# q and v of two pairs of heads in one load, a unit matrix copied on the chip, and a longer written order

## The chip, the cores and the metric

The kernel runs on one core of one Trainium2 chip. A core has five engines with a queue of instructions each: TensorE (PE, with its weight loads shown apart as PEld), VectorE (DVE), ScalarE (ACT), GpSimd (POOL) and SyncE (SP), which in this kernel issues all data transfers. Sixteen DMA engines move the data. Engines wait for each other through semaphores only, and each works through its own queue in order. The metric is the device time of one execution in microseconds (us).

## The reference

Three stages, one after the other, all in float32:

```python
# attention, B=4, H=8, S=576, D=64: heads 0-3 see the last 32 positions,
# heads 4-7 every fourth of the last 128
attn = softmax(where(mask, q @ k.T / 8, -1e9));  x = (attn @ v) as (2304, 512)
# soft mixture of 8 experts with 4 slots each
logits = x @ phi                                 # (2304, 32)
slots = softmax(logits, over tokens).T @ x       # (32, 512)
out_e = relu(slots_e @ w1[e]) @ w2[e]            # 8 experts, 512 -> 1024 -> 512
x = softmax(logits, over slots) @ out            # (2304, 512)
# gated layer
h = x @ w_in; out = (h * sigmoid(h)) @ w_out     # 512 -> 2048 -> 512
```

## The kernel before, in words

**Attention.** The 32 heads are worked off as 16 pairs n, the two heads of a pair on 64 partitions each. The loads of a pair are `lq`, `lk`, `lv`, each 128 rows of 576 floats (2304 B a row, 288 KB). POOL and DVE spread q into a block form (`qx`, `qy`) and mask v (`vx`, `vy`); PE puts the mask (`M`) and the scores (`S`) into PSUM; DVE takes the row maxima (`rm`), ACT the exponentials (`ex`, nine a pair), DVE the reciprocals (`rc`), POOL normalises (`nm`), DVE transposes in 32x32 blocks (`pt`), PE multiplies by v (`pv`). ACT copies the result out (`xe`), PE transposes it with a unit matrix (`T`) and computes the logits (`lt`), ACT stores x (`te`). q, v and k lie in slots that are used again: q in four, v in four (two towards the end), k in five, later three. A load into a slot waits until the spreading of the pair that was there is over.

**Experts.** After each fourth pair the running softmax over tokens is brought up to date (`da` to `ds`, `dc` its matrix products) and the softmax over slots prepared (`caa` to `cag`, then transposes `cb` on PE). After the last pair PE runs 16 steps `L1.i` over w1 and 16 steps `L2.i` over w2, each with a weight of 1 MB that a load `lw1.i` or `lw2.i` brings. The last of these, `L2.15`, is cut in three (`L2a`, `L2b`, `L2.15`: 256, 128 and 128 columns) with three loads.

**Gated layer.** The expert outputs (`soe`, `sotm`, `sote`) are multiplied with blocks of w_in (`aqh0`, `aq0` for the first 128 columns, `aqr0` for the next), copied out on ACT (`ah`) with a rest on DVE (`al`), and then `h` (PE), `gh` and `si` (ACT), `gl` (DVE), `on` and `om` (PE) run over the first third of the tokens; the other two thirds follow with `ch`, `cs`, `sh`, `sl`, `pp`. w_in and w_out come in a packed form that DVE unpacks (`cva`, `cvb`, `cvi`, and `cvc`, `cvd`, `cvo`). The first part of w_in is loaded in two halves (`lwi0.0`, `lwi0.1`).

**What sets the order.** Every step above is an operation with an engine, an estimated cost and a list of what it needs. All instructions are emitted in one order, and each engine gets its own in that order. The kernel before lets a list scheduler (`list_schedule`) find the order up to step `L2.5`, and takes the rest from the table `LATER`. The loads have an order of their own (`loads`, steered by the string `ATT`).

The change touches `qraw`, `vraw`, `load_q`, `load_v` (L126 to L184), the loop that declares the operations of a pair (L332 to L373), the load of the unit matrix (L1174, `cip`: 128 rows with phi and a float32 unit matrix side by side in tile `ip`), the list of loads (L1186 to L1199), `LATER`, and the layout of the inputs in `lay`.

Of the kernel before, what the change touches and what calls it, by code (L numbers as in the profile page):

```python
# [27 lines left out]
JH = 6  # L28
CBANK = ((2, 1), (5, 1), (4, 6), (5, 1))
# [3 lines left out]
def fused_kernel(ctx: ExitStack, tc: tile.TileContext, a: dict):  # L33
# [45 lines left out]
    def reg(key, off, n):  # L79
        return tiles[key][:, off:off + n]  # L80
# [38 lines left out]
    def before(slot, n):  # L119
        return max((m for m in range(n) if slot(m) == slot(n)), default=None)  # L120
# [47 lines left out]

    def load_q(n):
        b, p = divmod(n, 4)  # L170
        sp.dma_start(out=qraw(n), in_=a["q"][b, p])
# [160 lines left out]
    for n in range(NPAIR):  # L332
        b, p = divmod(n, 4)
        kb, rb = before(kslot, n), before(rslot, n)
        qb, vb = before(qslot, n), rb if n < NPAIR - 1 else None
        op(f"lk{n}", "SP", .74, [f"S{kb}"] if kb is not None else [], lambda n=n: load_k(n))
        op(f"lq{n}", "SP", .74, [f"qx{qb}", f"qy{qb}"] if qb is not None else [], lambda n=n: load_q(n))
        op(f"lv{n}", "SP", .74, [f"vx{vb}", f"vy{vb}"] if vb is not None else [], lambda n=n: load_v(n))
        for z in range(2):
            op(f"q{'xy'[z]}{n}", "DVE" if z and n not in QP else "POOL", .7, [f"lq{n}", f"S{n-2}" if n >= 2 else None], lambda n=n, z=z: spread(n, z))  # L340
        for z in range(2):
            op(f"v{'xy'[z]}{n}", veng(n) if z else "POOL", {"POOL": 1.4, "ACT": .68, "DVE": .745}[veng(n) if z else "POOL"], [f"lv{n}", f"pv{n-2}.1" if n >= 2 else "izm", ("nm0", "rc0")[z] if n == 1 else None], lambda n=n, z=z: vmask(n, z))
# [28 lines left out]
        op(f"T{n}", "PE", .56, ["cip", f"xe{n}", f"te{n-1}" if n else None], lambda n=n: tmm(n))  # L371
# [453 lines left out]
    op("ani", "ACT", .25, ["L2.6", "cip"], ani)  # L825
# [348 lines left out]
    op("cip", "SP", .37, [], lambda: sp.dma_start(out=ip, in_=a["ip"]))  # L1174
# [6 lines left out]
    op("crs", "POOL", .9, ["cip", "nm3"], crs)  # L1181
# [340 lines left out]
```

## Time and profile before

| | |
|---|---|
| median of 3 runs | 344.35 us (343.3 to 344.42) |
| the profiled execution | 343.64 us, its span from first to last instruction 341.5 us |
| granted TensorE clock | 1.000 of full speed |
| PE busy | 329.4 us, 96% of the span |
| DVE, ACT, POOL busy | 263.3, 221.9, 74.6 us |
| moved by DMA | 70.03 MB, nearly all in the first 145 us |

The span has three parts: attention until about 97 us, the experts until about 131 us, and the gated layer. The page's forty slices (8.5 us each) show the DMA engines full in slices 2 to 16, and PE nearly full throughout. A PE that is called busy is not always at its peak, since ends of matmuls are modelled. So an idle stretch of PE is a lower bound, and the weight loads (PEld), whose starts are measured, tell more exactly when PE had to wait. "[0.34 <-DMA x]" behind a row means that the engine stood idle for 0.34 us before it and that what came last was the transfer into x; "issue" means that it waited for nothing the profile shows.

### The profile page before, as it was taken

The page shows a single profiled execution, that of the slowest core. Times are in us where ns is not written, and L with a number is a line of the kernel's source. Part 1 is how long each engine was busy: PE and PEld are TensorE (multiplying, and loading weights), DVE is VectorE, ACT ScalarE, POOL GpSimd, SP SyncE. Part 2 cuts the span into 40 slices and gives each one's busy share as a digit, 9 for nine tenths or more (in the row PEclk, how much of TensorE's full clock was granted, in tenths as well). Part 3 has the DMA queues.
Part 4 walks back from the last instruction along what each step waited for, and adds up shares of the span by engine and source line. Part 5 has one row for each costly group of instructions (what it writes and reads, how often), then busy time and mean ns, then how long its engine had stood idle before and what let it go on. Part 6 is the DMA issues. An engine that isn't in the chain of part 4 may idle for free.

```text
span 341.5 us, 8179 instructions
## 1 busy us (share of the span) xinstructions
PE 329.4 (96%) x3221; PEld 272.1 (80%) x3232; DVE 263.3 (77%) x479; ACT 221.9 (65%) x639; POOL 74.6 (22%) x121
## 2 busy tenths in 40 slices
PE   7998999999899999999999999999999999999995
PEld 3687877777633337788888888999999999999995
DVE  5777877689660099999999997989994654999573
ACT  3599989797430125778496999996467666645540
POOL 6987978675260000000000000000000000000000
PEclk9999999999999999999999999999999999999999
DMA  7999999999999999818390000110200011000004
GB/s 259 405 405 406 403 401 407 416 404 415 416 405 423 416 411 419 349 58 322 125 356 15 0 0 2 55 68 2 77 3 0 0 71 69 3 23 23 2 22 147
DMA packets 17893, 70.03 MB, mean 205 GB/s; under 512 B 1984, under 2 KB 4288, under 8 KB 12096
## 3 DMA queue, kind: packets, MB, share of 16 engines
q1 hardware_dynamic: 17856, 69.53, 51.9%
q8 instruction: 25, 0.41, 0.5%
q14 instruction: 12, 0.10, 0.1%
HBM read 64.80 MB, written 4.72 MB: 204 GB/s over the span
## 4 chain that ended last, share of the span: by engine, by line
PE 83%; DMA 8%; DVE 3%; ACT 2%; POOL 1%; issue 1%; DVEq 0%; ACTq 0%; POOLq 0%
PE ps L86 80%; DMA w_w2.13_1760<-in_w 5%; PE ps L312 3%; DMA w_wi<-in_w_in 3%; ACT rt_px L232 1%; DMA rs_raw<-in_q 1%; POOL rv_v L1138 1%; ACT rt_px L301 1%; POOL rb_a L180 0%; PE ps L434 0%; POOL ra_a L180 0%; ACT x_xb L315 0%; DVE stats L227 0%; DVE csm L413 0%; DVE spaced L244 0%
## 5 line engine op out<-in xcount | busy, mean ns | idle before, releaser
L1083 DVE TENSOR_TENSOR rt_stl<-w_raww,rs_sth 128x768 fp32r<-128x768 f32 (+1 forms) x52 | 42.2, 830 | 18.2 <-ACT rs_sth L1081 17.9
L86 PE MATMUL ps<-w_ws,x_gz 128*128 128x512 f32 x216 | 53.6, 393 | 0.0
L86 PE MATMUL ps<-rs_sth,w_ws 128*128 128x384 f32 x192 | 53.1, 334 | 0.0
L1081 ACT CAST rs_sth<-w_raww 128x768 fp32r<-128x768 f32 (+1 forms) x52 | 37.8, 738 | 22.3 <-PE ps L86 16.6
L232 ACT ACTIVATE rt_px<-ps,spaced 128x64 f32<-128x64 f32 x144 | 43.5, 332 | 10.2 <-DVE spaced L228 8.5
L86 PEld LDWEIGHTS ps<-w_ws,x_gz 128*128 128x128 f32 x216 | 40.0, 188 | 7.7 <-issue 0.4
L86 PEld LDWEIGHTS ps<-rs_sth,w_ws 128*128 128x128 f32 x192 | 35.1, 188 | 0.0
L232 ACT ACTIVATION_READ_ACCUMULATOR rt_px<-ps,spaced 128x1 f32 x144 | 32.3, 225 | 0.0
L86 PE MATMUL ps<-rt_stl,w_ws 128*128 128x384 f32 x96 | 32.1, 334 | 0.0
L86 PE MATMUL ps<-ct_ct,rv_astk 128*128 128x384 f32 x96 | 27.3, 338 | 0.0
L1066 ACT ACTIVATE w_raww<-ps 128x384 f32<-128x384 f32 x48 | 22.0, 493 | 7.1 <-PE ps L86 7.0
L249 POOL TENSOR_TENSOR rt_px<-rt_px,stats 128x576 f32<-128x576 f32 (+2 forms) x17 | 18.6, 1093 | 8.2 <-DVE stats L245 3.4
L86 PEld LDWEIGHTS ps<-ct_ct,rv_astk 128*128 128x128 f32 x96 | 17.6, 188 | 2.4 <-issue 0.4
L86 PEld LDWEIGHTS ps<-rt_stl,w_ws 128*128 128x128 f32 x96 | 18.0, 188 | 0.0
L896 ACT ACTIVATE x_gz<-ps 128x768 fp32r<-128x768 f32 (+3 forms) x18 | 13.3, 740 | 4.8 <-PE ps L86 4.7
L899 DVE TENSOR_TENSOR x_gz<-rt_gtm,x_gz 128x768 fp32r<-128x768 f32 (+3 forms) x18 | 15.5, 864 | 1.0 <-ACT rt_gtm L889 0.9
L1081 ACT CAST rs_sth<-x_rawx 128x768 fp32r<-128x768 f32 x12 | 10.0, 837 | 9.6 <-PE ps L86 6.3
L889 ACT ACTIVATE rt_gtm<-ps 128x768 f32<-128x768 f32 (+3 forms) x18 | 13.2, 742 | 3.8 <-PE ps L86 3.6
L86 PEld LDWEIGHTS ps<-ra_a,rv_v 128*64 128x64 f32 x320 | 13.3, 137 | 2.8 <-issue 1.1
L86 PE MATMUL ps<-ra_a,rv_v 128*64 128x96 f32 (+2 forms) x320 | 14.9, 241 | 0.4 <-DVE ra_a L263 0.3
L1083 DVE TENSOR_TENSOR rt_stl<-x_rawx,rs_sth 128x768 fp32r<-128x768 f32 x12 | 11.5, 954 | 4.7 <-ACT rs_sth L1081 4.6
L315 ACT COPY x_xb<-ps 128x640 f32<-128x640 f32 x16 | 11.3, 708 | 5.7 <-PE ps L312 3.5
(298 smaller groups left out, 772.2 us busy)
## 6 DMA issues: line engine op xcount, KB each, us to landing
w_wi<-in_w_in SPq DMA_DIRECT2D x7, 1024.0 KB, 7.1
rs_wo<-in_w_out SPq DMA_DIRECT2D x4, 1024.0 KB, 5.8
rk_k<-in_k SPq DMA_DIRECT2D x12, 288.0 KB, 7.6
w_wo<-in_w_out SPq DMA_DIRECT2D x3, 1024.0 KB, 4.7
rs_raw<-in_v SPq DMA_DIRECT2D x9, 288.0 KB, 9.4
rs_raw<-in_q SPq DMA_DIRECT2D x8, 288.0 KB, 6.5
w_more<-in_q SPq DMA_DIRECT2D x8, 288.0 KB, 9.4
w_more<-in_v SPq DMA_DIRECT2D x6, 288.0 KB, 8.0
```

Source lines behind the costliest of these rows:

```text
L86: pe.matmul(out, lhsT=lhsT, rhs=rhs, start=start, stop=stop, skip_group_check=True)
L232: act.activation(out=preg(n)[:, j, :], in_=sj(n, j), func=ACTF.Exp, scale=D ** -0.5, bias=nmx[:, r, j // 3, j % 3:j % 3 + 1], accum_out=su ...
L249: pool.tensor_tensor(out=p, in0=p, in1=rinv[:, n % 2, j0:j1].rearrange("p (j o) -> p j o", o=1).to_broadcast([128, j1 - j0, 64]), op=ALU.mult)
L301: act.copy(out=x, in_=src)
L312: pe.transpose(ps[0:m, c:c + 128], x[:, 128 * t:128 * t + m], ident)
L315: act.copy(out=xreg(n)[:, :, 0:128], in_=ps[:, TC:TC + 640].rearrange("p (t c) -> p t c", c=128))
L889: act.activation(out=cols(gt(f), x), in_=hbs(x), func=ACTF.Silu)
L896: act.activation(out=cols(gbuf(f, 0), x), in_=hbs(x), func=ACTF.Silu)
L899: dve.tensor_tensor(out=gsl(gbuf(f, 1), x), in0=gsl(gt(f), x), in1=gsl(gbuf(f, 0), x), op=ALU.subtract)
L1066: op(f"cs{x}", "ACT", .385, [f"ch{x}", *d], lambda c=c, b=b, i=i, s=s: act.activation(out=at(c, b, i), in_=bank[6 + s][:, 0:TW], func=ACTF ...
L1081: op(f"sh{x}", "ACT", cost(c, PRODS[p][0], j, .42, .74), [*src, old, "cvo14" if o < 0 else None], lambda c=c, p=p, j=j: both(c, p, j, 0, l ...
L1083: lambda c=c, p=p, j=j: both(c, p, j, 1, lambda x, h, l: dve.tensor_tensor(out=l, in0=x, in1=h, op=ALU.subtract)))
```

## The change

1. q of pairs 2n and 2n+1 lie side by side in the input, 128 rows of 4608 B. From pair 2 on one load brings both, into two neighbouring slots; it waits until both are free. The same for v of pairs 2 to 13. Pairs 0 and 1, and v of pairs 14 and 15, are still loaded alone. That makes 7 double loads of q and 6 of v in place of 26 single ones.
2. The float32 unit matrix is no longer loaded. `cip` brings phi alone (128 rows of 512 B instead of 1024 B), and a new step `idn` on DVE copies the bfloat16 unit matrix, which comes with the mask, into float32.
3. `LATER` holds the whole order but for its first 37 operations, those of the start. The order of the loads comes from it as well.

```diff
+VLAST = NPAIR - 2
...
-    def qraw(n):
+    def qraw(n, m=1):
         i = qslot(n)
-        return reg("raw", 576 * i, 576) if i < 2 else reg("more0", 576 * (i - 2), 576)
+        return reg("raw", 576 * i, 576 * m) if i < 2 else reg("more0", 576 * (i - 2), 576 * m)
...
+    def lead(n, last):
+
+        return n if n < 2 or n >= last else n - n % 2
+
+    def load_two(raw, src, n, last):
+
+        x, y = src[n // 2], raw(n)
+        if lead(n + 1, last) != n:
+            sp.dma_start(out=y, in_=x[:, S * (n % 2):S * (n % 2) + S])
+        else:
+            sp.dma_start(out=raw(n, 2), in_=x)
+
     def load_q(n):
-        b, p = divmod(n, 4)
-        sp.dma_start(out=qraw(n), in_=a["q"][b, p])
+        load_two(qraw, a["q"], n, NPAIR)
...
     def load_v(n):
-        b, p = divmod(n, 4)
-        sp.dma_start(out=vraw(n), in_=a["v"][b, p])
+        load_two(vraw, a["v"], n, VLAST)
...
-        op(f"T{n}", "PE", .56, ["cip", f"xe{n}", f"te{n-1}" if n else None], lambda n=n: tmm(n))
+        op(f"T{n}", "PE", .56, ["idn", f"xe{n}", f"te{n-1}" if n else None], lambda n=n: tmm(n))
...
-    op("cip", "SP", .37, [], lambda: sp.dma_start(out=ip, in_=a["ip"]))
+    op("cip", "SP", .21, [], lambda: sp.dma_start(out=ip[:, 0:128], in_=a["phi"]))
+    op("idn", "DVE", .2, ["cmask"], lambda: dve.tensor_copy(ident, identb))
...
 LATER = """
-L2.5 cb2.1 cbs2.1 L2.6 ht1 lwo1 cb2.0 hr1 L2.7 lwi0.0 cvc0 L2.8 L2.9 cvd0 caf3 lw2.14 cvc1 L2.10 cva0.0 lw2.15 lw2b L2.11 ani L2.12 cvo0
...
+ex0.0 lw1.0 ex0.1 M1 lk3 ex0.2 S1 rm1 lq4 ex0.3 ex0.4 fl2 ex0.5 ex0.6 vx0 ex0.7 lk4 ex1.0 rc0 ex1.1 ex1.2 qy2 qx2 ex1.3 lv2 vy1 ex1.4 ex1.5
...
+    pairs = lambda x: np.ascontiguousarray(x.reshape(NPAIR // 2, 2, 128, S).transpose(0, 2, 1, 3)).reshape(NPAIR // 2, 128, 2 * S)
+    out["q"] = pairs(heads(inputs["q"]).transpose(0, 1, 2, 4, 3))
```

The order of SP's loads, in the first 20 us of the program. `in_q` and `in_v` are the inputs, `rs_raw` and `more0`, `more1` hold the slots, `in_w1` is the first expert weight (1 MB each). Before, from the eighth load on:

```order
L171 DMA w15_more0_115<-in_q 128x576
L167 DMA rk_k_110<-in_k 128x576
L184 DMA rs_raw_112<-in_v 128x576
L171 DMA w15_more0_115<-in_q 128x576
L167 DMA w15_more0_115<-in_k 128x576
L171 DMA rs_raw_112<-in_q 128x576
L167 DMA w16_more1_116<-in_k 128x576
L184 DMA w16_more1_116<-in_v 128x576
L171 DMA rs_raw_112<-in_q 128x576
L167 DMA rk_k_110<-in_k 128x576
L530 DMA ct_w1.0_283<-in_w1 128x2048
```

And now, from the eighth load on, with the line numbers of the changed file:

```order
L180 DMA w15_more0_115<-in_q 128x1152
L168 DMA rk_k_110<-in_k 128x576
L178 DMA rs_raw_112<-in_v 128x576
L544 DMA ct_w1.0_196<-in_w1 128x2048
L168 DMA w15_more0_115<-in_k 128x576
L180 DMA rs_raw_112<-in_q 128x1152
L168 DMA w16_more1_116<-in_k 128x576
L180 DMA w16_more1_116<-in_v 128x1152
```

Loads of q and v have 1152 columns, and the first 1 MB weight has moved ahead of k of pair 3, q of pairs 4 and 5, k of pair 4 and v of pairs 2 and 3.

PE's order at the change from the experts to the gated layer. The rows are, before: `L2.14`, `L2a`, `L2b` with `L2.15`, `cb3.1` (two rows), `sotm`, then `aqh0`, `aq0` and `aqr0` in one row (32 products), `h` for two blocks, `on`:

```order
L86 MATMUL ps<-w_w2.14_1819,x_sip 32x512 x4
L86 MATMUL ps<-w_w2.15_1828,x_sip 32x256 x4
L86 MATMUL ps<-w_w2.15_1828,x_sip 32x128 x8
L434 MATMUL ps<-ip,cc 128x128
L434 MATMUL ps<-ip,cc 128x64
L86 MATMUL ps<-s_62,x_sip 128x32 x4
L86 MATMUL ps<-w_wif_1826,lg 32x128 x32
L86 MATMUL ps<-ct_ct,rv_astk 128x384 x2
L86 MATMUL ps<-rk_ws_1843,x_gz 128x512 x4
```

Now:

```order
L87 MATMUL ps<-w_w2.14_1765,x_sip 32x512 x4
L87 MATMUL ps<-w_w2.15_1776,x_sip 32x256 x4
L87 MATMUL ps<-w_w2.15_1776,x_sip 32x128 x8
L448 MATMUL ps<-ip,cc 128x128 x3
L87 MATMUL ps<-s_62,x_sip 128x32 x4
L87 MATMUL ps<-w_wif_1796,lg 32x128 x16
L87 MATMUL ps<-ct_ct,rv_astk 128x384
L87 MATMUL ps<-w_wif_1796,lg 32x128 x16
L448 MATMUL ps<-ip,cc 128x128
L448 MATMUL ps<-ip,cc 128x64
L87 MATMUL ps<-rk_ws_1835,x_gz 128x512 x4
```

The first `h` product (`ct_ct,rv_astk`) stands between `aq0` and `aqr0`, and the larger transposes `cb3.0` have changed places with `cb3.1`.

## Rows read from the trace of the kernel before

**Rows 1.** The page: PE's busy time, and slices of PE, DMA and rate.

```profile
PE 329.4 (96%) x3221; PEld 272.1 (80%) x3232; DVE 263.3 (77%) x479; ACT 221.9 (65%) x639; POOL 74.6 (22%) x121
...
PE   7998999999899999999999999999999999999995
...
DMA  7999999999999999818390000110200011000004
GB/s 259 405 405 406 403 401 407 416 404 415 416 405 423 416 411 419 349 58 322 125 356 15 0 0 2 55 68 2 77 3 0 0 71 69 3 23 23 2 22 147
```

**Rows 2.** The chain of waits: start us, length us, what; 79 us to the end.

```profile
79.50 0.76 DVE csm L413
...
80.91 0.42 PE ps L86 x2
...
95.33 0.35 DVE x_sip L513
95.68 0.16 DVE acc L467
...
96.66 6.26 PE ps L86 x56
...
102.94 15.57 DMA w_w2.13_1760<-in_w
...
118.52 10.18 DMA w_wi<-in_w_in
...
130.12 0.70 DVE w_wif L638
...
130.87 1.47 PE ps L86 x33
...
134.21 203.75 PE ps L86 x1167
```

**Rows 3.** Timeline, 125 to 133 us: start, length, engine, line, operation [idle before].

```profile
125.26 0.13 PEld L86 LDWEIGHTS ps<-w_w2.14_1819,x_sip 128*32 128x32 f32 x4 [0.30 <-issue]
...
126.16 0.13 PEld L86 LDWEIGHTS ps<-w_w2.15_1828,x_sip 128*32 128x32 f32 x4 [0.34 <-DMA w_w2.15_1828<-in_w]
...
127.48 0.16 PEld L86 LDWEIGHTS ps<-w_w2.15_1828,x_sip 128*32 128x32 f32 x8 [0.37 <-DMA w_w2.15_1828<-in_w]
...
129.41 1.08 PE L86 MATMUL ps<-w_wif,lg 128*32 128x128 f32 x32
...
130.56 0.27 ACT L780 CAST rv_astk<-ps 128x128 fp32r<-128x128 f32 x1 [0.83 <-PE ps L86]
130.85 0.29 DVE L783 TENSOR_TENSOR rv_astk<-ps,rv_astk 64x128 fp32r<-64x128 f32 x1
...
130.87 1.08 PE L86 MATMUL ps<-w_wif,lg 128*32 128x128 f32 x32 [0.38 <-DVE w_wif L638]
...
132.69 1.19 PE L86 MATMUL ps<-rk_ws,x_gz 128*128 128x512 f32 x4 [0.19 <-ACT x_gz L896]
```

**Rows 4.** DMA packets of 20 to 60 us, when q, k, v and weights come mixed.

```profile
DMA packets 4845, 16.13 MB, mean 403 GB/s; under 512 B 540, under 2 KB 540, under 8 KB 3798
```

**Rows 5.** DMA packets of 84 to 97 us, when only weights come.

```profile
DMA packets 738, 5.42 MB, mean 417 GB/s; under 512 B 79, under 2 KB 79, under 8 KB 79
```

**Rows 6.** Busy time by stretch: us, PE, PEld, DVE, ACT, POOL, clock, DMA share, GB/s.

```profile
10.00:97.00 87.00, 81.46 (x1598) 64.01 (x1608) 68.00 (x191) 68.34 (x321) 63.30 (x99) 1.00 1.03 408
97.00:128.00 31.00, 30.90 (x294) 10.76 (x286) 11.48 (x26) 6.88 (x15) 4.07 (x6) 1.00 1.01 413
```

**Rows 7.** Timeline of DVE: the first row maximum, and a copy of 128x128.

```profile
6.36 0.76 DVE L227 TENSOR_REDUCE stats<-ps 128x9 f32<-128x576 f32 x1 [0.34 <-PE ps L86]
...
96.31 0.29 DVE L518 COPY x_sip<-ps 128x128 f32<-128x128 f32 x1
```

**Rows 8.** The page, DMA issues: count, KB each, median us from issue to landing.

```profile
rs_raw<-in_v SPq DMA_DIRECT2D x9, 288.0 KB, 9.4
...
w_more<-in_q SPq DMA_DIRECT2D x8, 288.0 KB, 9.4
```

More of the change, by code (lines that the diff above doesn't have):

```diff
@@ L824, in fused_kernel @@
                 op(f"ac{f}.{r}", "ACT", .31, [f"ah{q}" if r < 2 else f"al{q}"], lambda f=f, r=r: ac(f, r))
-    op("ani", "ACT", .25, ["L2.6", "cip"], ani)
+    op("ani", "ACT", .25, ["L2.6", "idn"], ani)
     for f in range(16):
@@ L1179, in crs @@
             pool.tensor_copy(s4[32 * g:32 * g + 32], eye)
-    op("crs", "POOL", .9, ["cip", "nm3"], crs)
+    op("crs", "POOL", .9, ["idn", "nm3"], crs)
     wl_ = [f"lw1.{i}" for i in range(16)] + [f"lw2.{i}" for i in range(16)] + ["lw2b", "lw2c"]
@@ L1187, in fused_kernel @@
     loads = ["lq0", "lk0", "cmask", "lq1", "lk1", "cip", "lv0", "lq2", "lk2", "lv1"]
-    vs = [f"lv{n}" for n in range(2, NPAIR)]
+    vs = [f"lv{n}" if lead(n, VLAST) == n else None for n in range(2, NPAIR)]
     n = 3
@@ L1191, in fused_kernel @@
         if c == "q":
-            loads += [f"lq{n}", f"lk{n}"]
+            loads += ([f"lq{n}"] if lead(n, NPAIR) == n else []) + [f"lk{n}"]
             n += 1
         else:
-            loads.append({"w": wl_, "v": vs, "i": il, "o": ol}[c].pop(0))
+            loads += [x for x in [{"w": wl_, "v": vs, "i": il, "o": ol}[c].pop(0)] if x]
     assert n == NPAIR and not vs + wl_ + il + ol
@@ new lines @@
+da0 la0 lw1.4 nm5 pv4.1 M7 vy5 xe4 ex6.2 pt5.0 S7 pt5.1 pt5.2 ex6.3 dt0 T4 pt5.3 qy8 vx5 ex6.4 qx8 pv5.0 ex6.5 lw1.5 ex6.6 lt4 te4 lk9 pv5.1
+lq10 ex6.7 rm7 dm0 rc6 dq0 ex7.0 ex7.1 ex7.2 db0 qy9 ex7.3 ex7.4 dsub0 dex0 nm6 xe5 ex7.5 pt6.0 lw1.6 qx9 ex7.6 vx6 pt6.1 vy6 dr0 dc0 M8
+ex7.7 ex7.8 S8 pt6.2 rc7 pt6.3 rm8 vy7 T5 nm7 te5 pv6.0 ex8.8 ex8.0 lv8 ex8.1 pt7.0 pv6.1 ex8.2 ex8.3 qy10 pt7.1 pt7.2 xe6 M9 ex8.4 ex8.5
+pt7.3 S9 T6 rm9 ex8.6 lq12 lk10 lk11 lw1.7 ex8.7 rc8 ex9.0 te6 ex9.1 ex9.2 ex9.3 vx7 ex9.4 lt5 qx10 vy8 pv7.0 pv7.1 vx8 nm8 qx11 M10 ex9.5
@@ new lines @@
+cbs3.0 lwi1.0 sotm0 sotm1 sote0 lwo2 sote1 aqh0 aq0 ah0 cvi0.1 al0 h0.0.0 aqr0 lwi2.0 cb3.1 gh0.0.0 cva1.0 gh0.0.1 on0.1.0 on0.2.0 ahr0
+cvb1.0 alr0 h0.0.1 si0.0.0 si0.0.1 cbs3.1 cvi1.0 h0.1.0 gl0.0.0 cvc2 on0.0.0 gh0.0.2 si0.0.2 aq1 gl0.0.1 ah1 cvd2 h0.1.1 on0.3.0 gh0.1.0
+gl0.0.2 ac2.0 lwi3.0 om0.0.0 ac2.1 am1 si0.1.0 al1 om0.1.0 cvo2 gl0.1.0 ac2.2 ac2.3 on0.5.0 on0.4.0 wh2 ac3.3 om0.2.0 cva3.0 cva2.0 om0.3.0
+om0.4.0 wl2 om0.5.0 h0.2.0 h0.2.1 om0.0.1 si0.2.0 om0.1.1 om0.2.1 om0.3.1 om0.4.1 gh0.2.0 ac3.2 on0.1.2 ac3.1 cvb2.0 cvb3.0 on0.0.2 ac3.0
@@ L1485, in lay @@
     out["mask"] = np.concatenate([mask, np.eye(128, dtype=np.float32)], 1).astype(bf)
[L1486 to L1489 removed]
+    out["phi"] = np.ascontiguousarray(inputs["moe_phi"].reshape(4, 128, NS).transpose(1, 0, 2)).reshape(128, 128)
     w1 = inputs["moe_w1"].reshape(E, 4, 128, 2, 512).transpose(3, 0, 2, 1, 4)
```

140 lines of the change are left out of this document (77 added, 63 removed).

## The prediction

> **What bounds the kernel now.** The page comes first: PE is busy 329.4 of 341.5 us, and the DMA engines are full from slice 2 to slice 16, some 9 to 137 us, at 401 to 423 GB/s [rows 1]. So there are two candidates until about 130 us and one after it. The chain of waits tells them apart: from 134.21 us it is one PE piece of 203.75 us, in which nothing of this change can shorten the work; from 102.94 to 128.70 it is two transfers, a second-layer weight of 15.57 us and the second half of the first w_in of 10.18 us, and then DVE unpacks (until 130.82) and PE starts at 130.87 [rows 2]. But PE was not idle meanwhile: from 97 to 128 us it was busy 30.90 of 31 us [rows 6]. A chain that names a DMA therefore does not say that 25 us are to be had. The two run side by side and finish nearly together, and the timeline shows by how much DMA is the later one [rows 3]. A step of 512 columns takes 0.9: seven of them (56 products, eight a step) fill the 6.26 us from 96.66 on [rows 2], and `L2.14` at 125.26 is followed by the next weight load at 126.16. The three parts of `L2.15` have 256, 128 and 128 columns, so 0.45, 0.22 and 0.22; unhindered the third would start at 126.16 + 0.45 + 0.22 = 126.83. It starts at 127.48, with a DMA named before it: PE lost 0.65 us to loads that were late. At 130.87 PE idled 0.38 more for the unpacked w_in, which hangs on the transfer that landed at 128.70. DMA is thus the later of the two by 0.65 + 0.38 = 1.03 us, and behind it PE binds. In attention, from 10 to 97 us, PE is busy 81.46 of 87 us [rows 6]: 5.5 us idle, held by chains over ACT, DVE and POOL, not by DMA.
>
> **The change part by part.** The sum is made against the profiled execution, 343.64 us; the median of the runs is 344.35, so 0.7 above it, and a difference carries over.
>
> *Double loads.* What a row costs an engine follows from two stretches. From 84 to 97 us only rows of 8192 B came: 738 - 79 = 659 packets in 13 us on 16 engines, 13,000 x 16 / 659 = 316 ns a row [rows 5]. From 20 to 60 us there were 4845 - 3798 = 1047 of these and 3798 - 540 = 3258 of 2304 B [rows 4]: (40,000 x 16 - 1047 x 316) / 3258 = 95 ns. A straight line through both has a slope of (316 - 95) / (8192 - 2304) = 0.0375 ns a byte and an intercept of 95 - 86.4 = 8.6 ns a row. A row of 4608 B should then take 181 ns in place of 190. Thirteen double loads join 13 x 128 = 1664 pairs of rows: 1664 x 8.6 / 16 = 0.9 us. No row of 4608 B occurs, so the bounds are: nothing, if the cost goes by bytes alone or a long row is cut in two; 1.3 us, if a long row went at the rate of the 8192 B rows (2 x 95 - 316 x 4608 / 8192 = 12 ns a pair). I take 0.9, the value of the line, which lies between.
>
> *Unit matrix.* 128 rows lose 512 B: 128 x 512 x 0.0375 / 16 = 0.15 us less transfer. The copy `idn` has no equal among the rows; the nearest is a DVE copy of 128x128 out of PSUM in 0.29 [rows 7], and I bound it by 0 and 0.5. It needs only the mask tile and stands ahead of the first row maximum, before which DVE idles 0.34 for PE [rows 7]; so it is hidden. Without that cover it puts off the first `rm` by 0.3, behind which `vy0` and `rm` of pair 1 are queued. Its first reader, `T0`, comes some 12 us later. Taken: 0.
>
> *What of it reaches the end.* All loads up to the second half of w_in end about 0.9 + 0.15 = 1.05 us sooner, provided that the DMA engines are never dry. The lateness in front of PE is 1.03. So the 0.65 at `L2.15` and the 0.38 both go: -1.03.
>
> *Order at the hand-over.* PE now has `h` ahead of `aqr0` (the order of PE in the section on the change). `aq0` ends at 129.41 + 1.08 = 130.49; `h` needs ACT's copy (130.56 + 0.27) and DVE's rest (130.85 + 0.29 = 131.14) [rows 3]. With that chain at its lengths PE idles 131.19 - 130.49 = 0.70. Queued behind `h` on PE is `aqr0`, which then hides what `on` used to wait for, 0.19 [rows 3]. Net +0.51. The 0.38 counted above is inside this new wait, so DVE's unpacking has 0.3 us of air there.
>
> *Order in attention and experts.* All instructions but the 37 first are placed anew; PE has as many as before, so only its idle time can change: 5.5 us at most, and the like amount in the bad direction. Two places speak for a gain. At 79.50 to 80.91 the chain leaves PE for DVE, where the maximum that the running softmax needs stands behind three steps of the other softmax (0.76 the longest) [rows 2]; `LATER` now names that maximum (`dm2`) far ahead of these steps (`cad0`). At 95.33 DVE clears a tile for 0.35 before the step PE waits for [rows 2]; now that step (`ds3`) goes first. Together up to 0.76 + 0.35 = 1.1. Against this stand waits that nobody has seen yet: `pv1.1` now comes soon after `te0`, `dr0` and `dc0` soon after `dsub0`, and any of them may cost some tenths. Bounds -1.5 and +1.5; I take -0.5.
>
> *Sum.* -1.03 + 0.51 - 0.5 = -1.0 us. One cap: if PE comes to `L2.15` 0.5 us sooner, the loads would have to be sooner by 1.15 for all of it to count, and they are by 1.05; that 0.1 is less than the working can resolve. So 342.6 for the profiled execution, and 343.3 from the median.
>
> **A rule weighed.** Rows 4 and 5 give 8.6 ns for a row, which is 8.6 x 128 / 16 = 69 ns for a load of 288 KB, whatever part of it belongs to the load and not to its rows. By the Trainium skill, page "DMA: Bandwidth & Descriptors", section on the anatomy of one DMA, a transfer takes about 2.0 us plus its bytes at 436 GB/s. If the engines paid this for each transfer, thirteen fewer would save 13 x 2.0 = 26 us. The trace does not agree: at 403 GB/s with mixed loads there is no room for 2 us between them. The page itself lays most of the 2 us to the wait for the last write's receipt.
>
> **The rivals.**
>
> *A: the new waits eat it.* The wait of `h` costs its 0.70 and attention gains nothing or loses a little: -1.03 + 0.51 + 0.3 = -0.2, 344.1. For it: the order is new in a thousand places, and PE's idle share there is small already. Against it: the two places named.
>
> *B: both gain in full.* DMA -1.2, and attention gives its 1.1, with the hand-over at +0.5 and no new waits: -1.8, 342.5. For it: the DMA engines are busy without a gap [rows 6], so every nanosecond saved there counts. Against: the cap named in the sum.
>
> *C: the DMA engines run dry, and it is slower.* A double load waits until two slots are free, four slots are now two, and SP works in order, so k, v and weights behind it wait too. What covers this is the backlog: a load lands 9.4 us after its issue (median) [rows 8], of which some 7 are queue. The point from which it decides is a stall of SP longer than that. Thirteen double loads with 0.2 us of dry engines each would put the end of the loads at -1.05 + 2.6 = +1.5 and the kernel at about +1.5, 345.9, since DMA is the later one as it is. For it: the first 1 MB weight now stands ahead of four small loads, so that v of pairs 2 and 3 lands later by 128 x 316 / 16 = 2.5 us and by two more pairs' worth (2 x 128 x 95 / 16 = 1.5), and the first pair of each double load comes 128 x 95 / 16 = 0.76 us later, with the second one's rows [rows 4, 5]. Against: rows 6 show the engines full, with no sign of a margin near zero. That a first pair can't be used alone is what the Trainium skill states on the same page, section on why a DMA increments its semaphore by 16: only the full count means that all data has landed.
>
> *D: it doesn't do what it says.* If the hardware cuts a row of 4608 B into two, only the 0.15 of the unit matrix is saved, most of the wait at `L2.15` stays, the wait of `h` (0.70) takes the place of those for w_in and of `on` (0.38 + 0.19), and attention gives its 0.5: -0.15 + 0.13 - 0.5 = -0.5, 343.8.
>
> **How the numbers follow.** What a measurement of this kernel can tell from no change is 0.3%, 1.03 us, so the border to "faster" lies at 343.32. The forecast, -1.0 with its own range from -1.7 to -0.4, has 0.47; A 0.19, B 0.21, C 0.10, D 0.03. The forecast lies on the border, half of it on either side. Faster: 0.235 + 0.21, so 0.45. Same: 0.235 + 0.19 + 0.03, so 0.45. Slower: 0.10. The range goes from 341.9 (B with half a us more from attention) to 344.8 (A with the unfavourable half of attention's bound), and leaves out most of C and the far end of B.
>
> **What would show it.** The page after should have 1664 packets fewer for q and v, and the mean rate from 20 to 60 us should be up by 1 to 2%. The weight loads before `L2.15` should show "issue" and no DMA, and the third part should start 0.90 + 0.45 + 0.22 behind `L2.14`. Before `h` of the first block there should be a wait for DVE's rest of 0.6 to 1.0 us on PE or PEld, and none before `on`. The start of the first expert step, 96.66 before, should come at 95.8 to 96.6 with one transpose group moved behind it. I am wrong in the mechanism if the engines show dry stretches before 120 us, or if DMA is still named in front of `L2.15`; and wrong in size if PE's idle time from 10 to 97 us is more than 6 us or less than 4.

## The result: slower by 0.75%, and the profile after

The changed kernel takes 346.07 us (median of 6 runs, 345.83 to 347.9), the kernel before in the same session 343.71 (6 runs, 343.0 to 344.42). The ratio is 1.0075, 95% interval 1.0051 to 1.0099: 2.4 us slower, where 343.3 with a range of 341.9 to 344.8 was forecast.

The page of the changed kernel, the lines that answer to [rows 1]:

```profile
PE 332.8 (96%) x3221; PEld 272.9 (79%) x3232; DVE 261.7 (76%) x480; ACT 221.0 (64%) x639; POOL 74.2 (21%) x121
...
PEclk9999999999989999999999999999999999999999
DMA  7999999999969999944644001020010020001004
GB/s 259 407 417 410 410 408 415 411 414 416 387 266 396 403 385 424 388 178 142 237 171 181 2 0 61 2 91 2 0 46 2 23 70 33 13 2 45 2 0 167
DMA packets 16021, 69.97 MB, mean 202 GB/s; under 512 B 1776, under 2 KB 4080, under 8 KB 10224
```

The transfers of 20 to 60 us, beside [rows 4]:

```profile
DMA packets 3484, 16.46 MB, mean 411 GB/s; under 512 B 385, under 2 KB 385, under 8 KB 2319
```

There are 1872 packets fewer than the 17893 of before (1664 rows and 208 small ones, 16 a load), and the rate is 2% higher, as forecast. In the same stretch of the trace a packet of 4608 B took 180 ns (median), where the prediction's line gave 181. The copy of the unit matrix is hidden, too (DVE's timeline, beside [rows 7]): DVE waits for PE behind it.

```profile
6.04 0.23 DVE L1189 CAST ip<-hsb 128x128 f32<-128x128 bf16 x1
7.24 0.76 DVE L238 TENSOR_REDUCE stats<-ps 128x9 f32<-128x576 f32 x1 [0.97 <-PE ps L87]
```

But on the page the twelfth slice (95 to 104 us) has 266 GB/s, and PE's clock dips there. The stretches, to be set beside [rows 6] (columns as there):

```profile
10.00:97.00 87.00, 80.54 (x1594) 63.15 (x1599) 65.20 (x184) 68.42 (x326) 60.67 (x96) 1.00 1.02 410
97.00:128.00 31.00, 30.12 (x248) 10.10 (x252) 9.68 (x30) 5.58 (x14) 6.33 (x9) 0.94 0.91 356
...
98.00:102.00 4.00, 4.00 (x20) 1.10 (x24) 1.36 (x7) 1.14 (x4) 2.26 (x3) 0.58 0.58 244
102.00:104.00 2.00, 2.00 (x24) 0.61 (x20) 0.25 (x2) 0.00 (x0) 0.46 (x1) 0.98 0.44 70
```

PE idles 6.46 us from 10 to 97 us, not 5.54, and the DMA engines run partly dry from 98 to 104 us (244 and 70 GB/s). What holds PE up just before, the chain of waits tells (start us, length us, what), where the chain of [rows 2] went from `dc3` straight to 95.33:

```profile
94.35 0.16 DVE chi L431
...
94.56 1.96 another core or an unknown queue
...
96.54 0.49 DVE cc L432
97.03 0.39 DVE acc L407
...
97.48 0.34 DVE acc L481
...
97.87 0.33 PE ps L519
```

DVE stands for 1.96 us before it writes `cc` (step `caf1`), and the profile can't name what ended the wait. The weight loads of PE (timeline) show it:

```profile
94.51 0.82 PEld L87 LDWEIGHTS ps<-x_xb,le 128*32 128x32 f32 x32 [0.32 <-ACT le L475]
95.54 0.15 PEld L87 LDWEIGHTS ps<-x_xb,le 64*32 64x32 f32 x8 [0.20 <-issue]
95.89 0.11 PEld L87 LDWEIGHTS <-cc 128*128 128x128 bf16 x2 [0.20 <-issue]
97.86 0.14 PEld L519 LDWEIGHTS ps<-ip,acc 128*128 128x128 f32 x1 [1.86 <-DVE acc L481]
```

The row at 95.89 is the fill step `ff1`, two matmuls whose result nobody reads; they take their operands from `cc`. It is emitted ahead of `caf1`, so `caf1` may overwrite `cc` only when `ff1` is done, and on PE `ff1` stands behind the 40 products of `dc3`. Behind `caf1` on DVE are queued `dacc3` (L407) and `ds3` (L481), and for `ds3` PE waits 1.86 us before `sit` (L519). Before, `ff1` (93.07) stood ahead of `dc3` (93.70) on PE, and DVE wrote `cc` at 93.80 without a wait (timeline of the kernel before):

```profile
93.07 0.11 PEld L86 LDWEIGHTS <-cc 128*128 128x128 bf16 x2
...
93.70 0.82 PEld L86 LDWEIGHTS ps<-x_xb,le 128*32 128x32 f32 x32 [0.51 <-ACT le L461]
93.80 0.49 DVE L418 TENSOR_TENSOR cc<-cn,chi 128x320 f32<-128x320 f32 x1
...
95.88 0.14 PEld L505 LDWEIGHTS ps<-ip,acc 128*128 128x128 f32 x1 [0.24 <-DVE acc L467]
```

From `dc3` to `sit` it is 97.86 - 94.51 = 3.35 us, before 95.88 - 93.70 = 2.18.

At the hand-over to the gated layer (timeline, beside [rows 3]):

```profile
129.95 0.13 PEld L87 LDWEIGHTS ps<-w_w2.14_1765,x_sip 128*32 128x32 f32 x4 [0.30 <-issue]
...
131.23 0.78 PEld L87 LDWEIGHTS ps<-w_w2.15_1776,x_sip 128*32 128x32 f32 x20 [0.30 <-issue]
...
134.93 0.27 ACT L794 CAST rv_astk<-ps 128x128 fp32r<-128x128 f32 x1 [0.83 <-PE ps L87]
135.23 0.30 DVE L797 TENSOR_TENSOR rv_astk<-ps,rv_astk 64x128 fp32r<-64x128 f32 x1 [1.77 <-ACT rv_astk L794]
...
135.58 0.44 PE L87 MATMUL ps<-ct_ct,rv_astk 128*128 128x384 f32 x1 [0.71 <-DVE rv_astk L797]
```

No DMA is named before `L2.15`, whose parts run through as one group of 20 weight loads, and `h` waits 0.71 us for DVE's rest. Both are as forecast. But `L2.14` starts at 129.95 in place of 125.26. Of this, 1.6 us is a fallen clock in this one execution: from the first expert step to `L2.14` it took 31.17 us, and 29.55 at full clock with the same order there (fill_behind).

The profiled execution took 347.9 us, the other five 345.8 to 346.3. In the profiled one PE's granted clock was 0.50 (1.2 GHz of the two levels) from 99 to 102 us, after PE had been busy 0.42 of the 2 us before 98; the text below compares medians, or steps ahead of 98 us.

### The profile page after: what moved, and what is told of

The parts are those of the page before. It is cut to its first block, busy times and chain, and to the rows that moved or that the text cites. A ratio compares the mean times of both kernels' runs of the same rounds, so it can differ in the third digit from the quotient of the medians.

```text
span 346.1 us, 8167 instructions
## 1 busy us (share of the span) xinstructions
PE 332.8 (96%) x3221; PEld 272.9 (79%) x3232; DVE 261.7 (76%) x480; ACT 221.0 (64%) x639; POOL 74.2 (21%) x121
## 4 chain that ended last, share of the span: by engine, by line
PE 89%; DVE 4%; ACT 3%; issue 1%; POOL 1%; another core or an unknown queue 1%; DVEq 0%; ACTq 0%; POOLq 0%
PE ps L87 86%; PE ps L323 2%; ACT rt_px L243 2%; DVE stats L238 1%; PE ps L448 1%; DVE cc L432 0%; ACT rt_px L312 0%; ACT rt_px L310 0%; POOL rv_v L208 0%; POOL rb_a L192 0%; ACT x_xb L326 0%; POOL rt_px L260 0%; ACT x_gz L910 0%; DVE spaced L255 0%
## 5 line engine op out<-in xcount | busy, mean ns | idle before, releaser
L87 PE MATMUL ps<-rb_a,rv_v 128*64 128x96 f32 (+2 forms) x320 | 15.1, 242 | 1.9 <-issue 1.1
L87 PEld LDWEIGHTS ps<-rb_a,rv_v 128*64 128x64 f32 x320 | 13.2, 137 | 4.6 <-issue 2.1
L238 DVE TENSOR_REDUCE stats<-ps 128x9 f32<-128x576 f32 x16 | 11.8, 739 | 6.6 <-PE ps L87 3.4
L87 PE MATMUL ps<-ra_a,rv_v 128*64 128x96 f32 (+2 forms) x320 | 14.2, 242 | 0.2 <-issue 0.2
```

What stands on the lines that cost most here:

```text
L87: pe.matmul(out, lhsT=lhsT, rhs=rhs, start=start, stop=stop, skip_group_check=True)
L238: dve.tensor_reduce(out=mxs[:, n % 2], in_=ps[:, c:c + 64 * NJ].rearrange("p (j c) -> p j c", c=64), axis=AXX, op=ALU.max)
```

## The experiments

Each ran beside the kernel before on the same chip. Ratios are to that kernel, with 95% intervals; its median was 343.6 to 343.8 us in every session.

**fill_behind.** The order on each engine stays. `ff1` is emitted behind the writers of `cc`, so that it waits for them, and not they for it.

```diff
-... dc3 ff1 caf1 dwe3 cag1 dacc3 ds3 sit ...
+... dc3 caf1 dwe3 cag1 ff1 dacc3 ds3 sit ...
```

> The changed kernel with one step emitted later: the fill matmuls ff1 now stand behind cag1 in the written order, so that they read tile cc after DVE and POOL have written it, and not before. The order on PE, DVE, ACT and POOL is unchanged word for word. Theory 1 (the lost time is a wait that the order made: DVE's write of cc had to wait for ff1, which stood behind dc3 on PE): the 1.96 us wait of DVE before that write goes, sit starts 1.1 to 1.5 us sooner (about 96.5 in place of 97.86), the first expert step at 97.3 to 97.7 in place of 98.78, and the whole time falls by 1.1 to 1.4 us against the changed kernel, to 1.3 us above before (ratio 1.003 to 1.005). Theory 2 (the end is set by the loads, whose engines ran dry between 97 and 110 us): sit comes sooner all the same, but a DMA is named before L2.15 or the unpacked w_in is late, and the whole time falls by less than 0.4 us (ratio 1.006 or more).

Measured: 344.77, ratio 1.0035 (1.0021 to 1.0049), 1.3 us less than the changed kernel. DVE's timeline:

```profile
93.97 0.23 DVE L431 CAST chi<-cn 128x160 fp32r<-128x160 f32 x1
94.31 0.49 DVE L432 TENSOR_TENSOR cc<-cn,chi 128x320 f32<-128x320 f32 x1
...
95.74 0.35 DVE L481 SCALAR_TENSOR_TENSOR acc<-ps,wgt,acc 128x129 f32<-128x129 f32 x1 [0.48 <-PE ps L87]
```

The wait is gone, `sit` starts at 96.14 and the first expert step at 97.04, a little sooner than theory 1 said, since `dc3` came 0.29 sooner in this execution. The clock stayed at 0.998 or more in all five runs. Theory 1 holds: this wait is half of the loss.

**rest_first.** At the hand-over `aqr0` goes ahead of `h` again, as before.

```diff
-... ah0 cvi0.1 al0 h0.0.0 aqr0 lwi2.0 ...
+... ah0 cvi0.1 al0 aqr0 h0.0.0 lwi2.0 ...
```

> The changed kernel with one swap at the hand-over undone: aqr0 is again emitted ahead of h0.0.0. Theory 1 (the wait of h for DVE's rest costs what the sum said): aqr0 runs in that wait, 0.3 to 0.5 us faster than the changed kernel (ratio to before 1.006). Theory 2 (what is saved before h comes back as a wait before on, or before the first om): the same time as the changed kernel within 0.2 us (ratio 1.007 to 1.008).

Measured: 345.87, ratio 1.0067 (1.0054 to 1.008), 0.2 less than the changed kernel; the intervals overlap, so the times settle neither theory. The traces tell more: from `aqh0` to the next 16 products with w_in it is 5.36 us here and 5.58 in the changed kernel, so the swap costs some 0.2 there.

**both_fixes.** The two edits above together.

> The changed kernel with both steps put right: ff1 emitted behind cag1, and aqr0 ahead of h0.0.0. Theory 1 (two waits that add up): 1.2 + 0.2 = 1.4 us faster than the changed kernel, 0.9 to 1.1 us above before (ratio 1.0025 to 1.0032). Theory 2 (with PE sooner, the loads become the later ones again, and aqr0 waits for the unpacked w_in whatever the order): as fill_behind, 1.2 us above before (ratio 1.0035).

Measured: 344.64, ratio 1.0027 (1.0016 to 1.0038), on theory 1, though the interval doesn't shut out theory 2 (1.0035). In the trace the same stretch is 5.36 us again, and 5.57 in fill_behind. Some 0.9 us above before are left.

**loads_alone.** `LATER` names all operations, in the order of before on PE, ACT, DVE and POOL; a load stands as early as its needs allow.

```diff
-ex0.0 lw1.0 ex0.1 M1 lk3 ex0.2 S1 rm1 lq4 ex0.3 ex0.4 fl2 ...
+... qx1 lq4 lk4 lv2 lk5 lw1.0 lw1.1 lw1.2 ex0.0 vy0 M1 ex0.1 vx0 S1 ...
```

> Double loads of q and v and the unit matrix copied on chip, with PE, ACT, DVE and POOL in the order of the kernel before, word for word (idn placed behind it1 on DVE). Theory 1 (the order is what costs; the loads do what the sum said): the wait before the third part of L2.15 (0.65) goes or falls under 0.2, the unpacked w_in is in time, 0.7 to 1.0 us faster than before (ratio 0.997 to 0.998). Theory 2 (double loads wait for two slots, and the pairs' data come late): PE idles more from 10 to 97 us than the 5.5 us of before, the first expert step comes later than 96.66 and the kernel is 1 us or more slower than before (ratio 1.003 or more).

Measured: 345.44, ratio 1.0053 (1.0038 to 1.0069): theory 2. SP's issues and the stretch behind them (windows):

```profile
26.45 0.33 SPq L168 DMA_DIRECT2D w_more<-in_k  x1
36.30 0.33 SPq L180 DMA_DIRECT2D rs_raw<-in_v  x1
```

```profile
30.00:34.00 4.00, 3.14 (x66) 2.48 (x67) 2.60 (x8) 3.65 (x15) 2.70 (x5) 1.00 1.03 417
34.00:38.00 4.00, 4.00 (x85) 3.21 (x82) 3.80 (x11) 3.23 (x20) 3.78 (x6) 1.00 0.70 220
```

SP stood 9.5 us before a double load of v (pairs 8 and 9), for the slot that its second half needs; 4 x (1 - 220/417) = 1.9 us of transfer were lost. It stood again before v of pairs 12 and 13, with 354 GB/s from 52 to 58 us, 6 x (1 - 354/417) = 0.9 us more. That is rival C's mechanism, in two places in place of thirteen, and about at its price (2.6 us dry). The changed kernel doesn't have it: there the mean from 30 to 90 us is 412 GB/s.

**order_alone.** The code of before; each double load becomes two single ones at its place.

> The kernel before (single loads, unit matrix loaded) with the written order of the changed kernel; each double load is replaced by two single loads one behind the other at its place. Theory 1 (the order costs and the loads gain nothing behind it, since PE comes later than the loads): as slow as the changed kernel within 0.4 us, 2.0 to 2.6 us above before (ratio 1.006 to 1.0075). Theory 2 (the double loads are what costs): within 0.5 us of before (ratio under 1.0015). Theory 3 (the loads gain their 1.0 us in any order): 3.0 to 3.6 us above before (ratio 1.009 to 1.0105).

Measured: 347.82, ratio 1.0124 (1.0099 to 1.0149), above all three. Three of the six runs had a mean clock of 0.995 and took 348.5 to 349.2, the other three 346.6 to 347.1, some 3.1 us above before, where theory 3 stands: by these, the loads and the unit matrix gain some 0.7 in this order. In this order the single loads are late in attention: `dc3` starts at 95.25, in the changed kernel at 94.51.

**attention_alone** and **attention_clean.** The changed order up to `dt3`, that of before behind it; the second moves three steps at the seam, where the two orders meet (`caa2`, `cae1`, `la3`).

```diff
-... dt3 caa2 cb0.0 cae1 la3 ff0 dm3 dq3 db3 dr3 dsub3 lw2.5 ff1 ...
+... dt3 cb0.0 ff0 dm3 la3 dq3 cae1 db3 dr3 dsub3 caa2 lw2.5 ff1 ...
```

> Double loads, unit matrix copied on chip, and the written order of the changed kernel up to and with dt3; from there on all engines in the order of the kernel before (so ff1 ahead of dc3, cb1.0 ahead of L1.0, aqr0 ahead of h0.0.0). Theory 1 (the loss lies in the order behind dt3, above all in the wait of DVE for ff1; the double loads in the new attention order give their 1 us): dc3 comes 0.5 to 0.8 us later than before, the wait of 0.65 before the third part of L2.15 and the 0.38 before aqr0 go, in all 0.5 us faster to 0.2 us slower than before (ratio 0.9985 to 1.0005). Theory 2 (the attention order loses as much as the whole change): 1.5 us or more above before (ratio 1.0045 or more).

> attention_alone without the seam that it had behind dt3: DVE does dm3 ahead of la3 and caa2, and POOL dq3 ahead of cae1, as in the changed kernel (in attention_alone dr3 came 0.35 us later for it); the rest as there. All thirteen double loads, the changed kernel's order in attention, the order of before behind it. Theory 1 (the written order in attention costs 0.4 to 0.8 us at dc3, and the loads give 0.4 + 0.1 back at L2.15 and aqr0): 0.3 us faster than before to 0.1 slower (ratio 0.999 to 1.0003), and the whole rest of the 2.4 us lies in the order behind dt3. Theory 2 (dm3 was not what dr3 waited for): as attention_alone (ratio 1.0004 to 1.001).

Measured: 343.89 and 343.84, both 1.0004 (0.9995 to 1.0013, 0.9995 to 1.0012). So without the changed order behind `dt3` nearly all of the 2.4 us is gone, with the double loads still in. But `dr3` stayed late, as theory 2 of the second had it, so DVE's steps were not the seam (PE has `cb0.0` between `dt3` and `ff0` in both; that this is the seam is not shown).

**attention_clean_ds3.** `ds3` moves ahead of `sipy`.

> attention_clean with ds3 ahead of sipy on DVE. Theory 1 (PE binds from dt3 on, the loads being early enough): sit and the first expert step 0.2 to 0.35 us sooner, and the end by as much, 0.2 to 0.6 us faster than before (ratio 0.9983 to 0.9994). Theory 2 (the loads of the second layer follow PE and are the later ones): no faster than attention_clean within 0.1 us.

Measured: 343.7, 1.0002 (0.9994 to 1.0011): not to be told from the one before, and not the gain of theory 1. In the trace the first expert step starts 2.79 us behind `dc3`, 2.95 in attention_clean.

**tail_alone.** Before up to `dt3`, the changed order behind it, single loads.

> The kernel before (single loads) in its own order up to and with dt3, and from there on in the written order of the changed kernel. Theory 1 (the loss lies behind dt3): DVE waits about 1.9 us for ff1, sit comes 1.0 to 1.3 us later than before, no DMA is named before L2.15 since PE comes later than the loads, in all 1.4 to 2.0 us above before (ratio 1.004 to 1.006). Theory 2 (it lies in attention): under 0.7 us above before (ratio under 1.002).

Measured: 346.47, 1.0082 (1.0063 to 1.0102), above theory 1. Three executions took 345.6 to 345.9, as it said, and three 347.1 to 347.8, two of these with a mean clock of 0.993 and 0.995; the profile is of the one at full clock (347.08). There `sit` came 1.45 later, where 1.0 to 1.3 was expected, and `L2.15` waited for its loads again, since these are held up too: the load of second-layer weight 8 needs a place that PE's first steps free, and is issued 2.0 us behind the start of `L1.0` in this kernel (100.21) and in before (98.65).

**one_pair_single** and **late_pair_single.** One double load of v taken back.

```diff
+ALONE = (6, 7)        # late_pair_single: (8, 9)
-        return n if n < 2 or n >= last else n - n % 2
+        return n if n < 2 or n >= last or (last == VLAST and n in ALONE) else n - n % 2
```

> loads_alone with one of the thirteen double loads taken back: v of pairs 6 and 7 comes in two loads again, at the places in SP's queue where the kernel before has them; all else as in loads_alone. Theory 1 (in loads_alone SP stood 9.5 us before this load, longer than the 7 us of backlog, and the engines ran dry; nothing else was wrong with the double loads): no stretch under 380 GB/s between 30 and 45 us, the loads end about 0.97 us sooner than before, 0.5 to 0.9 us faster than before (ratio 0.9974 to 0.9985). Theory 2 (another double load stalls SP as long): dry engines somewhere else from 40 to 60 us, and no faster than before (ratio 1.000 or more).

> loads_alone with v of pairs 8 and 9 in two loads again (the double load before which SP stood from 26.8 to 36.3 us there); all else as in loads_alone. Theory 1 (with the stall gone the 1 us that double loads save comes to the end): no second under 380 GB/s from 30 to 97 us, the waits of 0.65 before L2.15 and 0.38 before aqr0 go, 0.6 to 1.0 us faster than before (ratio 0.997 to 0.9983). Theory 2 (from the load of second-layer weight 8 on, each load waits for a step of the first layer on PE to free its place; what is saved before 92 us is given back as dry engines from 98 to 102 us): the stall is gone, engines dry by 0.7 to 1.2 us from 98 to 102, and the end moves by less than 0.4 us (ratio 0.999 to 1.001). Theory 3 (another double load stalls SP): dry engines from 34 to 60 us and slower than before (ratio 1.002 or more).

Measured: 344.77, 1.0033 (1.002 to 1.0047), and 344.95, 1.0029 (1.0012 to 1.0045). The first took back the wrong pair: the load that SP stood before was v of pairs 8 and 9, and the stall stayed. The second has no dry stretch at 34 us, but one behind the double load of v of pairs 12 and 13, which SP issued at 52.74, 8.1 us behind the load ahead of it. That is its theory 3 (windows of late_pair_single):

```profile
50.00:52.00 2.00, 1.93 (x50) 1.54 (x48) 1.57 (x6) 2.00 (x12) 1.73 (x4) 1.00 1.02 412
52.00:58.00 6.00, 5.37 (x107) 4.47 (x110) 5.17 (x15) 5.55 (x28) 4.95 (x7) 1.00 0.81 263
```

**less_traffic.** The kernel before without the loads of k of pairs 13 to 15 (it leaves out data that the result needs, and serves only to time the rest).

> The kernel before, single loads and its own order, with the loads of k of pairs 13, 14 and 15 left out (the three pairs compute with what lies in their slots, so the output of attention is not the reference's): 3 x 128 rows of 2304 B, some 2.3 us of the 16 engines less, between 61 and 75 us, and nothing else. Theory 1 (loads saved in attention come to the end, as the sum had it): the third part of L2.15 and aqr0 no longer wait, 0.8 to 1.0 us faster than before (ratio 0.997 to 0.998). Theory 2 (they are given back where loads wait for PE's first-layer steps): engines dry by 1.5 us or more from 92 to 102 us, the wait before L2.15 stays above 0.4, and the end moves by less than 0.4 us (ratio 0.999 to 1.001).

Measured: 343.41, 0.9986 (0.9972 to 1.0), between the theories. `L2.15` has no wait left, the weight loads of the second layer's end being one group again, and `aqr0` 0.28 in place of 0.38:

```profile
125.17 0.13 PEld L86 LDWEIGHTS ps<-w_w2.14_1816,x_sip 128*32 128x32 f32 x4 [0.30 <-issue]
...
126.46 0.78 PEld L86 LDWEIGHTS ps<-w_w2.15_1825,x_sip 128*32 128x32 f32 x20 [0.30 <-issue]
```

The third part starts 1.83 us behind `L2.14` (127.00), where [rows 3] have 2.22; `aqr0` 0.99 behind `aq0`, where it was 1.09. So the loads were late by 0.39 + 0.10 = 0.49 us; with PE where it was, more than that is not to be had from traffic. (The twelve executions fall into two groups, 342.2 to 343.1 and 343.7 to 344.3, and the profile is of the first; what parts them is open.)

**two_moves.** The two gains that the prediction named, alone, in the kernel before.

```diff
-... rm15 pv13.0 ... rc14 lv15 ex15.0 cad0 ... dt2 ... dm2 ...  dc3 ... sipy sipz cb1.1 ds3
+... rm15 dt2 pv13.0 ... rc14 lv15 ex15.0 dm2 cad0 ...  dc3 ... ds3 sipy sipz cb1.1
```

> The kernel before, single loads, with three steps moved and nothing else: dt2 on PE ahead of pv13.0 and dm2 on DVE ahead of cad0 (the maximum of the second softmax ahead of three steps of the other), and ds3 ahead of sipy on DVE. These are the two gains of the order that the sum named, 0.76 and 0.35. Theory 1 (they are real): dc3 comes 0.5 to 0.8 us sooner, the first expert step 0.8 to 1.1; the loads are the later ones by then and cap it, so 0.1 to 0.5 us faster than before if the loads follow PE (ratio 0.9985 to 0.9997). Theory 2 (the chain has another branch as long, on ACT or POOL): the first expert step comes less than 0.4 us sooner and the end not at all (ratio 0.9995 to 1.0005).

Measured: 343.71, 1.0 (0.9989 to 1.001). The first expert step starts at 95.94 (before 96.66), and the third part of `L2.15` at 127.46 (before 127.48): PE came 0.72 sooner and waited for the loads.

**moves_and_loads**, late_pair_single with these moves.

> late_pair_single with the three moves of two_moves: double loads but for v of pairs 8 and 9, unit matrix copied on chip, and otherwise the order of the kernel before. Theory 1 (PE comes to the first layer sooner, so the loads behind it start sooner, and with fewer rows they are done sooner: the two need each other): 0.7 to 1.3 us faster than before (ratio 0.996 to 0.998). Theory 2 (either alone is all there is): no faster than the better of late_pair_single and two_moves within 0.2 us.

Measured: 344.32, 1.0026 (1.0012 to 1.004); SP stalls there as well, so it tells little of the two theories. In the trace `dc3` comes at 94.05, in late_pair_single at 93.76.

**few_pairs** and **few_pairs_moves.** `VLAST = 8`: ten double loads, in the order of before; the second with the three moves.

> Double loads only where SP did not stand long before them in loads_alone and late_pair_single: the seven of q and v of pairs 2 to 7; v of pairs 8 to 13 comes in single loads (ten double loads in place of thirteen), unit matrix copied on chip, and the order of the kernel before. Theory 1 (without a stall the rows saved come to the end, up to the 0.4 + 0.1 us by which less_traffic shows the loads to be late): no dry stretch from 30 to 97 us, 0.3 to 0.6 us faster than before (ratio 0.9983 to 0.9991). Theory 2 (any double load in this order stalls SP, the ones of q too): dry engines somewhere from 30 to 65 us, and not faster than before (ratio 1.000 or more).

> few_pairs with the three moves of two_moves (dt2 ahead of pv13.0, dm2 ahead of cad0, ds3 ahead of sipy). Theory 1 (PE 0.7 us sooner at the first layer, and loads that are 0.8 us sooner, so that it comes to the end): 0.6 to 1.0 us faster than before (ratio 0.997 to 0.9983). Theory 2 (the loads are given back as dry engines): no faster than few_pairs within 0.2 us.

Measured: 342.85, 0.9977 (0.9968 to 0.9986), and 342.42, 0.9966 (0.9954 to 0.9978), which is 1.3 us faster than before and 3.6 faster than the change. few_pairs gained 0.8, more than its theory 1 allowed: in its trace PE, too, came 0.64 sooner to the first expert step (96.02). The intervals of the two overlap, and with the moves this step came at 96.08, so that the moves add anything is not shown. Nor does a run part the double loads from the unit matrix and from the earlier places of the loads. Windows of few_pairs_moves, without a dry stretch:

```profile
30.00:97.00 67.00, 62.73 (x1245) 49.18 (x1253) 52.21 (x153) 52.18 (x237) 46.43 (x67) 1.00 1.02 410
97.00:102.00 5.00, 5.00 (x52) 1.52 (x48) 2.61 (x8) 3.02 (x7) 2.87 (x5) 1.00 1.01 411
```

## Why the prediction was wrong, step by step

**The step that failed: "Order in attention and experts ... Bounds -1.5 and +1.5; I take -0.5."** From the total, 2.4 + 0.49 (the loads, below) - 0.2 (the hand-over), it was about +2.7, outside its own bounds. It looked at two places that gain and at lists of needs, and said of PE "as many as before, so only its idle time can change". What it missed, by size:

- *The fill ahead of the copy, 1.3* (fill_behind). The sentence "now that step (`ds3`) goes first" is true and was worth nothing, because `ds3` itself had become late. The list of needs of `ff1` (`TAIL`: `dr3` and `te15`) doesn't name `cc`; the wait follows from the place of a read and a write of one tile in the written order. I had read PE's rows at the hand-over, not these: `dc3` and `ff1` have changed places on PE, and that is where the question "who writes what `ff1` reads?" had to be put.
- *The order of small steps among the expert steps, about 0.8.* The weight loads of fill_behind, then of attention_clean (which has the old order there), from `L1.0` on:

```profile
97.04 0.16 PEld L87 LDWEIGHTS ps<-ct_w1.0_196,x_sip 128*32 128x32 f32 x8 [0.23 <-DVE x_sip L532]
103.18 0.31 PEld L448 LDWEIGHTS ps<-ip,cc 128*128 128x128 f32 x3 [0.84 <-issue]
117.33 0.40 PEld L448 LDWEIGHTS ps<-ip,cc 128*128 128x128 f32 x2 [0.84 <-issue]
119.64 0.31 PEld L448 LDWEIGHTS ps<-ip,cc 128*128 128x128 f32 x3 [0.84 <-issue]
...
130.43 0.59 PEld L87 LDWEIGHTS ps<-w_wif,lg 128*32 128x32 f32 x24
```

```profile
97.95 0.16 PEld L87 LDWEIGHTS ps<-ct_w1.0_196,x_sip 128*32 128x32 f32 x8 [0.36 <-DVE x_sip L532]
118.12 0.40 PEld L448 LDWEIGHTS ps<-ip,cc 128*128 128x128 f32 x2 [0.84 <-issue]
120.39 0.39 PEld L448 LDWEIGHTS ps<-ip,cc 128*128 128x128 f32 x3
...
130.39 0.70 PEld L87 LDWEIGHTS ps<-w_wif,lg 128*32 128x32 f32 x28
```

  `aqh0` starts 33.39 us behind `L1.0` in the one and 32.44 in the other. `cb1.0` (103.18) has been moved from the gap before `L1.0` in among the expert steps, and `cb2.0` (119.64), which in the old order follows `ht1` without a gap (120.39), stands by itself behind one of 0.84. Of the 0.95, 0.13 came back ahead of `L1.0` (2.82 us from `dc3`, 2.95 in attention_clean). The windows call PE busy all through these steps, so a bound on its idle time could not hold this. It is read from the two traces; no run moved these steps alone.
- *Attention, about 0.7.* `dc3` starts 0.81 us later than before in the changed kernel, 0.52 in fill_behind, 0.41 in rest_first and 1.20 in both_fixes, which all have the same order up to there; so single executions differ by as much as the loss. It lies from 60 to 80 us, where PE idles 2.44 us (before 0.94). Of these, 1.07 are one stop of PE that the profile names no cause for (last section). It is 0.90 to 1.17 in all eight kernels with the changed order in attention, and in none of those with the old one. How much of the loss is this stop, and how much the new waits that the prediction feared, no run tells.

**The term of 1.03 us for the loads: half as large, and tied to PE.** The lateness was 0.49 (less_traffic). I had taken `L2.14` and the unhindered parts of `L2.15` as 0.90, 0.45 and 0.22, by their columns; between the starts of their weight loads the traces show 0.86, 0.65 and 0.33 where no load is late. And of the 0.38 before `aqr0`, 0.28 stays with the loads in time (less_traffic). "Provided that the DMA engines are never dry" failed twice. With the old order, two double loads of v stalled SP, as rival C said. With the new one, the stretch from 98 to 104 us is partly dry, because the next loads wait for PE's first expert steps: SP stood 9.3 us for PE before it issued second-layer weight 8 at 102.39. The fallen clock adds to this in the profiled execution; in rest_first, with the same wait at full clock, 100 to 102 us has 152 GB/s. PE late makes the loads late. It did not cost the changed kernel more, since no DMA is named before `L2.15`.

**The hand-over, +0.51: right in mechanism, too large.** `h` waited 0.71 (0.70 predicted), `on` no longer. By the times and ratios its cost is 0.1 to 0.3 (rest_first, both_fixes), less than the intervals can tell from nothing; in the traces it is some 0.2.

**The two gains named** (0.76 and 0.35) are shown only in part. The move of `ds3` gave 0.16 between `dc3` and the first expert step wherever it was made (2.80 in place of 2.96). The move of `dm2` brought `dc3` 0.55 sooner in two_moves, and no sooner in moves_and_loads and few_pairs_moves (94.05 against 93.76, 93.28 against 93.06). No run shows either at the end of the kernel.

**The rivals.** A (new waits eat the gain) names the kind of thing that came, with 0.8 us of them where some 2.9 came, at other places. D falls: a row of 4608 B went in 180 ns. C gave 345.9, near the result, by a mechanism that the changed kernel avoids, so that is luck; loads_alone showed it. Both signs that were to prove the prediction wrong appeared: dry engines before 120 us, and 6.46 us of idle PE, over the bound of 6.

**The rule weighed.** The 2.0 us a transfer stand in the Trainium skill, page "DMA: Bandwidth & Descriptors", section on the anatomy of one DMA, for transfers that GpSimd issues. Here SP issues them, so that "the trace does not agree" says more than it can. The sum didn't use this rule.

## What to carry to other kernels

When an order is rewritten, look at every pair of a reader and a writer of one tile that changes places across engines, fillers included: a step with no result can still hold a writer back. Price a late transfer against the same instructions run unhindered, not against a share of their columns. Where loads wait for slots, join only those whose two slots come free together, and look at what SP has queued behind them. Before a trace's times are compared over kernels, look at how far executions of one order differ (here 0.8 us at `dc3`).

## What the runs showed of the hardware

- A row of 2304 B took an engine 95 ns (median from 20 to 60 us before), one of 4608 B 180 (changed kernel), one of 8192 B 313 (both), so joining two short rows saved 6 to 10 ns (6 by the changed kernel's own 93 for a short row).
- PE's clock fell to its lower level (0.50 of full, 1.2 GHz) for 3 us after the 1.9 us wait before `sit` in the profiled executions of the changed kernel and of order_alone. By the mean clock (0.995 or less) it fell in one of six executions of the changed kernel, three of six of order_alone, two of six of tail_alone, and in none of fill_behind, nor of rest_first, which has the same wait. It fell without that wait, too: in three of eight of late_pair_single, whose profile shows 0.52 from 130.5 to 134 us, after PE had waited 0.5 to 1.1 us four times for loads. By the Trainium skill, page "TensorE: Matmul & The Clock Gate", section on the HAM clock gate, the gate goes by how busy PE was of late. The rows agree in that PE had waited ahead of each fall that a profile shows. A wait at a critical place can so cost twice.
- In all kernels with the changed order in attention PE stops at about the same product of `pv11.0` (behind 12 or 13 recorded ones) for nothing that the profile shows, as here in fill_behind (timeline):

```profile
68.20 0.79 PE L87 MATMUL ps<-rb_a,rv_v 128*64 128x96 f32 x13
69.89 1.23 PE L87 MATMUL ps<-rb_a,rv_v 128*64 128x96 f32 x27 [0.90 <-issue]
```

  A packet of the instruction queue, 16 KB, passes from 67.4 to 68.5 us, and PE goes on 1.4 us behind its end (1.3 to 1.5 in three others). But it had ended before PE stopped, and in the kernel before one passes at 67.0 to 68.1 without a stop. The Trainium skill, page "Advanced Engine Details and Errata", section on the ISA cache, gives cache lines of 16 KB, 256 instructions, which is the size of that packet. That PE waited for instructions is thus possible, and not shown.
